# Fifty-one words of a written-out instruction order change place, in a kernel of block-sparse attention and a squared-ReLU layer

## The chip, the cores and the metric

The kernel runs on one core of a Trainium2 chip. Five engines work side by side, each with a queue of its own: PE (TensorE, matrix products; its weight loads, PEld, overlap them), DVE (VectorE), ACT (ScalarE), POOL (GpSimd) and SP (SyncE, which here only issues transfers and reads registers). Transfers are done by 16 DMA engines. The metric is the device time in microseconds of one execution. Beside the median of the timed runs there is one profiled execution, from which all rows of the profile come.

## The reference

Attention over 4 batches, 8 heads, 768 positions and 64 dimensions, with a mask in blocks of 32 positions: each block of queries sees its neighbours, the first and the last block, and three sampled blocks of keys; the first and the last block of queries see all keys. Its output, 3072 rows of 512, goes through a layer with a squared ReLU.

```python
mask = np.abs(blk_i - blk_j) <= window
mask = mask | (blk_i == 0) | (blk_j == 0) | (blk_i == n_blocks - 1) | (blk_j == n_blocks - 1)
for qb in range(n_blocks):
    for kb in sampled_blocks[qb]:
        mask[qb*block:(qb+1)*block, kb*block:(kb+1)*block] = True
...
attn = attn / (np.sum(attn, axis=-1, keepdims=True) + 1e-09)
x = attn_out.transpose(0, 2, 1, 3).reshape(B * S, H * D)
h = x @ w_in            # 512 -> 2048
r = np.maximum(h, 0.0)
return (r * r) @ w_out  # 2048 -> 512
```

## The kernel before, in words

The work is cut into some 1200 tasks. A *unit* is a pair of heads of one batch (units 0 to 3 are batch 0, 4 to 7 batch 1, and so on); a *tile* of the layer is 256 rows of one batch, written (batch, first row, 256).

Batches 0 and 1 are done densely: a unit's queries and keys are loaded, cast to bf16 (`cast_qk`, `cast_v`, line 121 on ACT, 123 on DVE and POOL), transposed (`transp` on PE, or by a DMA transpose, `transp_dma`, line 312), multiplied (`scores`, by way of `pair`, line 203), exponentiated on ACT (`exps`, L357), masked on DVE (`masks`, L364), multiplied with the values (`values`) and normalized (`normalize`, L407 and L410). The result is transposed into `xT` by PE (`x_transp`, and `x_evac` copies it out of PSUM) or by DMA (`x_transp_dma`, L437).

Batches 2 and 3 are done sparsely, in six *visits* each. The value rows of a batch are stored to memory (`v_store`, L533, `rows<-VB`) and read back selected: a window and the edge blocks by plain transfers of SP (`v_window`, L547 and L551), sampled blocks by an indirect transfer of POOL (`v_gather`, L573). Keys are selected on chip by copies whose place comes from registers (`k_gather`, L588 to L594, on POOL or DVE). The registers are filled by a read of the table `tab` (`blocks_of`, L556, shown as TENSOR_LOAD): the first reads for POOL, DVE and SP are made at the end of `table_rows` (task 25), and each later one at the end of the `k_gather` or `v_gather` that has used up the one before it. Then `s_scores`, `s_exps` (L619), `s_masks` (L626), `s_values` (L649), `s_normalize` (L655, L658) and `s_transp` (L662) follow.

The layer of a tile is `hidden` (16 columns of 128 in four groups of four, each in four tasks), `relu` (L703 on ACT, L705 on DVE), `square` (L714 on ACT, L716 on POOL), and `output` in eight parts, followed by `out_copy` and `store`. The last tiles' outputs are split into narrower pieces.

The order is written out by hand. The string `PROGRAM` lists all tasks as words: the letter is the engine (P for PE, V for DVE, A for ACT, G for POOL, S for SP), then comes the task's number, and after a slash the PSUM cell (0 to 3) that its result takes. Each engine does its words in the order in which they stand; what stands between two words of one engine that belong to other engines fixes only the order in which buffers are handed out.

```python
for word in PROGRAM.split():
    i, _, spot = word[1:].partition("/")
    t = tasks[int(i)]
    ...
    t.fn(names[word[0]])
```

Buffers of a pool (`qc` for cast keys and queries, `pT` for exponentials, `r` and `g` for the layer, `ys` for outputs) rotate; a task waits for the last reader of the buffer that it takes. The transfers that SP issues go through eight completion counters in rotation, so a transfer also waits until the one eight places before it has landed.

Of the kernel before, what the change touches and what calls it, by code (L numbers as in the profile page):

```python
# [25 lines left out]
def kernel(  # L26
# [751 lines left out]
    def T_(f, *args, **kw):  # L778
        return Task((lambda e: f(*args, e)), **kw)
# [102 lines left out]
    def visit(b, v, vw, acts):  # L882
        gs_ = [g for g in VISITS[v] if g]
        vb, kb = Buf("vg"), Buf("kg")
# [76 lines left out]
    for T in TILES:  # L961
# [35 lines left out]
        V29 A32 V35 P30/2 P36/0 P0/3 V31 V37 A1 P33/2 V34 P11/3 G46 P100/3 P104/1 A101 V43 A105 P44/2 P102/0 V45 P47/3 A103 V57 V109  # L997
        V48 V54 P58/3 P111/1 V59 P55/3 A112 P113/2 V56 P115/0 V41 A114 P4/3 P9/3 P125/1 V67 G64 P2/3 A116 P106/2 V3 G52 A126 P5/3
        P123/3 V107 A124 G74 P108 P65/1 P121/0 V110 V66 G63 A122 P68/3 P82/1 P84/2 V69 P131/3 S18 V83 A85 S28 S19 S42 S53 S20 P135/0
        A132 V49 P86/2 P117/1 V87 G60 A136 G73 V118 P61/3 P133/2 V62 P90/0 G38 P119 A134 P127/3 V91 G75 P168/0 A120 P15/2 V128 P39/2  # L1000
        G76 P10/1 A169 P12/1 P174/1 V153 V40 P129 P137/2 G78 V130 A175 P144/0 G70 P88/3 V138 P147/1 A145 V176 P139 A89 P71/0 V140 V72
        A148 P171/3 V170 P779/2 P780 A172 V146 P92/1 P187/0 P781 V93 A188 P782 V173 P50/3 P181/1 A783 V189 P177/0 V51 A182 G784 P141/2
        P772/3 V178 P773 A142 V149 G79 P184/1 P179 P774 V207 V180 A185 G22 V143 P94/0 P775 V183 P155/2 A95 P150/1 V776 A156 G785
        P158/0 A159 P161/2 V151 P786/3 V186 P787 A162 P215/0 V157 P152 P788 A154 P14/2 V160 P789 A216 P98/2 P190/1 S80 V163 S251 A99
        V790 S252 P212/0 A777 P164/2 A213 V191 G791 P793/3 A778 V165 P794 S81 P209/0 G792 S259 P192 P166 P795 A210 V167 S260 P796 V193
        V294 V217 G77 P822/2 A797 P823 V214 P197/1 P194/0 G799 P824 A198 P825 P816/3 A195 G254 V826 P817 P226/1 A798 S255 P818 V196
        A227 P200/2 P810/0 V264 P811 S267 A201 V211 P243/1 P819 S265 V256 P812 A244 P218/2 V228 P813 S257 A820 V199 P219 P800/1 V220
        A814 S261 V202 P240/3 P221 P801 A241 V262 P96/0 S263 P802 A222 V97 A815 V242 P237/2 P223/3 S268 P203/0 A238 V245 P803 S275
        V272 A224 S332 S276 P229/2 P204 P804 V225 A230 S273 P805 G266 A821 V231 P286/2 P806 A287 V205 P232/3 V239 A827 P206 P289/2
        P233 V270 P807 A290 V208 S271 V234 P296/0 A808 P246/2 V291 P235 S253 P247 V236 A297 V288 S437 P299/1 P828/3 V248 P829 A300  # L1010
        V280 P302/0 P830 V278 A303 P249 P283/1 P831 V250 S279 V298 A284 P314/2 P850/0 V832 P851 S277 A315 P844/1 V304 S281 P845 A833
        P311/3 V285 P852 P853 V258 A312 P846 V301 S269 P847 A854 V316 P292/3 S21 P862/2 V313 A848 P293 P305/0 V295 P863 G282 A855
        P308/1 P306 G849 S454 P864 A309 V307 P353/3 S436 P865 A354 P326/0 P856/1 V866 P857 A327 P320/3 P858 V310 A321 P323/2 V274
        P834/0 V355 A324 S438 P859 V322 S445 P347/3 P835 A860 S383 S444 V328 P317/2 S460 A348 V325 P350/1 S809 P318 P836 V349 A351
        V319 P329/3 A867 P334/1 V352 P330 P837 A335 V331 G447 V23 P356/2 S333 A861 G439 P340/3 P838 A341 G441 P839 G459 P362/1 P337/3
        S452 P357 G443 P840 S442 A338 G449 P841 A363 S434 P868/3 S450 A842 P359/1 P869 V342 A360 S446 V339 P374/0 S843 P870 V345 A375
        V358 S462 V336 P377/1 S448 P365/2 P871 V361 A366 V364 P343/0 S461 A378 P371/2 V367 S453 P344 P872 V346 A372 V376 P368/1 P398/0
        V373 P401/2 P369 A399 P873 V379 A402 V370 S469 S440 P380/0 P391/1 P381 V403 A392 P385/2 P874 V382 A386 V400 S384 P388/0 P16/1
# [3 lines left out]
        V424 P395 S471 P416/1 P930/2 A417 P899 V397 P931 A895 P410/1 V900 P932 P933 A411 P902/0 V430 A934 V501 P475/1 P903 A476 P912/2  # L1022
        V418 P488/1 P904 V415 A489 V412 P431/3 A901 P480/1 P913 V477 S497 S604 P432 P914 S620 V433 A481 G635 P915 S614 V482 P419/1
        G502 A916 P485/3 S538 P905 A486 P420 A935 P490/3 P478/2 V421 P906 G498 V487 A491 S435 V544 P918/1 A479 P907 V492 G545 P473/3
        P483/2 P908 A474 S605 A484 P909 G615 A917 P919 P493/3 G499 A910 S911 G619 P506/0 S621 P920 V494 A507 P7/2 S540 S500 P512/2
        P921 A513 V508 P946/0 P947 A922 P509/3 P503/2 P948 A510 G522 P949 S622 P952/1 A504 S518 S543 V950 P552/3 P953 A923 G542 P936/2
        V514 S877 V511 P555/0 S496 P937 G541 V523 A556 P938 S616 A553 V505 P954 P546/0 P955 S521 A547 P939 V956 P515/3 V548 P524/0
        V557 P549/1 P940 A525 G587 V516 A951 P941 S517 A550 P942 G625 A957 V551 P527/1 P964/3 G519 S626 P965 A528 V554 P943 G617 V529
        P958/1 A944 P966 G607 P967 P959 V968 P530/0 P533/2 G623 P960 A531 S629 P961 V588 S583 S608 A534 P558/3 G520 A969 P992/2 S628
        V609 G565 P993 A962 S581 S618 P986/0 V559 P987 A963 P994 S610 V526 P592/1 P988 A593 P995 G627 P989 S606 A996 P970/1 V990 S561  # L1030
        S560 P998/3 G997 P589/2 V532 P999 A590 P971 P595/0 G562 P1000 A596 P972 V535 V566 G585 P1001 P536/2 G631 P980/0 A1002 V537
        P981 G584 P973 V633 S539 P982 G611 V597 P567/2 P983 S632 A568 P974 G563 A991 V984 P975 S586 A1003 P598/2 P976 S624 A599 P573/0
        P977 A574 V600 S636 V594 P1020/3 A985 S663 S564 P1021 V978 P570/2 P1026/0 A571 P1022 V591 S945 P1023 S665 S634 V640 P576/2
        P601/1 A577 V575 P1027 A1024 S637 P1004/2 V572 V602 A1025 P641/3 P1028 G666 V569 P1005 S603 A642 V578 G638 P1006 S639 P1032/3
        G669 P653/1 P1029 A654 P1033 A1030 P1007 P646/1 P1034 A647 P1035 P579/0 A1036 P1008 V580 A1031 P643/1 P656/3 V670 P1009 S582
        A657 P1010 A644 S706 S686 V645 P648/1 P1014/3 A649 P658/0 P1015 A659 P651/1 P1011 V660 A652 V655 V650 P1016 V690 A1012 P1017
        P661/0 A1018 S1013 G691 S979 A1037 S668 P680/1 P677/3 V662 P1048/2 G1019 A678 P1049 P1054/0 A681 V679 P674/3 P1050 A675 P1051
        G667 P1060/1 V1052 P1055 P671/3 G688 P1061 P1056 A1053 P1062 P1057 A672 P1038/2 V1058 P1063 P1066/3 V682 A1059 P1067 V673
        P692/0 P1039 V676 A1064 V712 P1068 A693 P683/1 A1065 G713 P1069 V684 S708 S664 P698/0 P1040 A699 G710 P1041 S749 S685 A1070
        V700 P720/0 P701/1 G1071 P695/3 S751 S687 P1042 A721 V733 A702 P1043 A696 P714/0 P1044 A715 P723/1 V694 P1045 G734 S711  # L1040
        P1088/3 A1046 P1089 P1082/0 S689 A724 P1083 P717/2 P1090 A718 G755 P1072/1 P1091 S1047 P1084 G709 V756 A1092 S752 P1094/2
        P1095 A1093 P1085 P1096 V1086 P1073 P1074 V703 V716 P1097 V719 P1100/3 V697 P1075 V1098 P704/0 V725 A1099 P1101 S729 V705
        P741/2 P1076 A742 V722 S707 P1102 P760/2 P1103 A761 P726/0 S732 A1087 P766/2 P1077 V727 A1104 P1078 V762 S728 A767 G1105 P1079
        V768 S754 P763/2 P735/0 P1106/3 A764 G730 A736 P1107 V737 G731 P744/0 P1108 V743 A745 V765 P1109 G753 A1080 P1130/0 P738/2
        P1116/1 A739 P1117 P1131 V740 P1118 V746 P757/2 P1119 A758 P1110 V1120 P747/2 V759 P1132 V748 P1133 P1137/1 V1134 S750 P769/2
        P1111 A1135 G1136 V770 P1138 G1122 S771 P1123/2 P1124 P1139 G1121 S1081 P1140 P1125 A1141 P1126 P1112 V1127 G1142 P1113 A1129
# [37 lines left out]
```

## Time and profile before

| what | us |
|---|---|
| median of 3 runs | 261.69 (261.49 to 263.17) |
| span of the profiled execution | 256.7 |
| median less span | 5.0 |
| PE busy | 242.0 (94%) |
| ACT busy | 186.2 (73%) |
| DVE busy | 166.8 (65%) |
| POOL busy | 95.7 (37%) |

The span runs from the first to the last instruction that the profile shows; the 5.0 us beside it lie around it. A row of waits reads: engine, line, what it waited for, the sum in us, how many times, the longest. A row of a timeline reads: start and length in us, engine, line, operation, what is written from what, how many instructions, and in brackets the idle time before it with what ended it. A row of the chain reads: start, length, what. A row of windows gives for each stretch its length and then, engine by engine, busy us and count, followed by the granted clock of PE as a share of full speed, the busy share of the DMA engines and the GB/s moved.

### The profile page before, as it was taken

To read this page: it belongs to the slowest core of one execution; us is meant where nothing else is said; L and a number is where in the kernel's file an instruction comes from. 1 tells how busy PE (TensorE), PEld (TensorE's weight loads), DVE (VectorE), ACT (ScalarE), POOL (GpSimd) and SP (SyncE) were. 2 spreads that over 40 slices of the span, in tenths; PEclk is the share of its full clock that TensorE was granted. 3 is DMA by queue.
4 is the path that set the end of the run, shared out by engine and by line. 5 is a ranking of instruction groups with operands and counts; after the bars stand their busy time and mean duration, and the time that the engine had idled before them with its cause. 6 is when DMAs were issued, how large, how long until landed. Compare 5 with 4: busy or idle time off the path is not lost.

```text
span 256.7 us, 12046 instructions
## 1 busy us (share of the span) xinstructions
PE 242.0 (94%) x5265; PEld 182.8 (71%) x5265; DVE 166.8 (65%) x390; ACT 186.2 (73%) x219; POOL 95.7 (37%) x193
## 2 busy tenths in 40 slices
PE   7988999999999997979999999989999999999993
PEld 4667889769876776856966776667866765777683
DVE  7677987879789986855375677366475665731300
ACT  3899999999998798858857857758777466244430
POOL 2274534020426014708437784162815307060200
PEclk9999999999999999999999999999999999999998
DMA  6999999999789999599999999981843556142031
GB/s 192 371 275 200 195 217 216 213 257 216 228 242 177 262 220 254 113 195 238 259 220 198 227 241 188 277 152 28 251 73 78 153 137 151 43 124 82 3 116 55
DMA packets 63509, 47.09 MB, mean 183 GB/s; under 512 B 31455, under 2 KB 58464, under 8 KB 63456
## 3 DMA queue, kind: packets, MB, share of 16 engines
q1 hardware_dynamic: 58320, 37.61, 65.9%
q0 software_dynamic: 4448, 8.25, 16.0%
q8 instruction: 41, 0.67, 1.1%
q10 hardware_dynamic: 688, 0.46, 0.6%
q14 instruction: 12, 0.10, 0.2%
HBM read 35.51 MB, written 7.91 MB: 169 GB/s over the span
## 4 chain that ended last, share of the span: by engine, by line
PE 66%; DVE 9%; DMA 7%; issue 5%; POOL 5%; ACT 4%; SPq 3%; DVEq 1%; POOLq 0%; ACTq 0%
PE X L203 59%; DMA QKT<-qc 5%; PE X L649 4%; POOL qc L123 2%; PE X L395 2%; DMA VG<-rows 2%; ACT pT L357 2%; POOL VG L573 2%; SPq L312 1%; DVE QKT L123 1%; SPq L151 1%; PE X L305 1%; ACT r L703 1%; DVE pT L364 1%; DVE qc L123 1%
## 5 line engine op out<-in xcount | busy, mean ns | idle before, releaser
L203 PE MATMUL X<-xT,w_in_sb 64*128 64x256 bf16 x1536 | 99.4, 269 | 1.8 <-ACT g L714 1.8
L203 PE MATMUL X<-w_out_sb,g 64*128 64x512 bf16 (+3 forms) x960 | 94.8, 333 | 0.1
L203 PEld LDWEIGHTS <-w_in_sb 64*128 64x128 bf16 x1536 | 74.0, 94 | 13.6 <-DMA xT<-XS 1.9
L357 ACT ACTIVATE pT<-X 128x1024 bf16<-128x1024 f32 x72 | 70.7, 1033 | 8.0 <-PE X L203 7.2
L203 PEld LDWEIGHTS <-g 64*128 64x128 bf16 x960 | 41.0, 94 | 26.8 <-PE X L203 0.4
L619 ACT ACTIVATE pT<-X 128x768 bf16<-128x768 f32 (+1 forms) x56 | 41.6, 765 | 21.8 <-PE X L203 20.8
L714 ACT ACTIVATE g<-r 128x1024 bf16<-128x1024 f32 (+1 forms) x44 | 40.3, 931 | 13.8 <-DVE r L705 13.7
L705 DVE TENSOR_SCALAR r<-X 128x1024 f32<-128x1024 f32 x22 | 26.9, 1224 | 24.7 <-PE X L203 23.2
L364 DVE TENSOR_TENSOR pT<-pT,VG 128x1024 bf16<-128x1024 bf16 x60 | 39.5, 692 | 3.2 <-ACT pT L357 2.4
L716 POOL TENSOR_TENSOR g<-r 128x512 bf16<-128x512 f32 (+1 forms) x16 | 20.9, 1316 | 47.8 <-DVE r L705 18.8
L626 DVE TENSOR_TENSOR pT<-pT,MKS 128x768 bf16<-128x768 bf16 (+1 forms) x48 | 28.3, 618 | 12.5 <-ACT pT L619 12.4
L703 ACT ACTIVATE r<-X 128x1024 f32<-128x1024 f32 x26 | 27.5, 1070 | 10.2 <-PE X L203 9.0
L203 PE MATMUL X<-QKT 64*128 64x256 bf16 (+1 forms) x384 | 32.5, 254 | 2.5 <-DMA QKT<-qc 1.6
L573 POOL DMA_INDIRECT VG<-rows,idx x20 | 20.0, 1000 | 19.7 <-DMA rows<-VB 9.4
L203 PEld LDWEIGHTS <-QKT 64*128 64x128 bf16 x384 | 16.9, 97 | 7.5 <-issue 3.6
L123 POOL CAST VB<-vs 128x768 bf16<-128x768 f32 x10 | 8.8, 888 | 27.3 <-DMA vs<-in_v_dram 21.3
L123 POOL CAST qc<-ks 128x384 bf16<-128x384 f32 (+1 forms) x17 | 9.3, 576 | 24.3 <-DMA ks<-in_k_dram 22.1
L203 PEld LDWEIGHTS <-pT 64*128 64x128 bf16 x768 | 16.1, 94 | 2.6 <-issue 0.2
L203 PE MATMUL X<-VB,pT 64*128 64x65 bf16 x768 | 17.1, 190 | 0.0
L203 PEld LDWEIGHTS <-KG 64*128 64x128 bf16 x528 | 13.2, 95 | 5.4 <-issue 1.8
L121 ACT COPY ys<-X 128x1024 f32<-128x1024 f32 (+2 forms) x11 | 9.9, 904 | 9.0 <-PE X L203 7.7
L203 PE MATMUL X<-QKT,KG 64*128 64x64 bf16 x528 | 14.8, 190 | 1.6 <-DVE XS L658 1.0
(104 smaller groups left out, 205.8 us busy)
## 6 DMA issues: line engine op xcount, KB each, us to landing
vs<-in_v_dram SPq DMA_DIRECT2D x14, 384.0 KB, 4.7
ks<-in_k_dram SPq DMA_DIRECT2D x13, 384.0 KB, 4.8
qs<-in_q_dram SPq DMA_DIRECT2D x12, 384.0 KB, 4.8
out_dram<-ys SPq DMA_DIRECT2D x9, 512.0 KB, 4.9
VG<-rows SPq DMA_DIRECT2D x20, 132.0 KB, 5.1
w_in_sb<-in_moe_w_in_dram POOLq DMA_DIRECT2D x2, 1024.0 KB, 9.2
w_out_sb<-in_moe_w_out_dram POOLq DMA_DIRECT2D x4, 512.0 KB, 8.4
rows<-VB SPq DMA_DIRECT2D x2, 792.0 KB
```

The lines of the kernel that those rows point to most:

```text
L123: (V if e == "DVE" else G).tensor_copy(out=out, in_=in_)
L203: last = nc.tensor.matmul(out(r ^ crossed), lhsT(r ^ crossed, rows), rhs(r ^ crossed, rows), skip_group_check=True, **kw)
L357: A.activation(out=pT[:, :, 0:n], in_=stile.pop(a)[:, :, 0:n], func=AF.Exp, scale=scale)
L364: V.tensor_tensor(out=pT, in0=pT, in1=m[:, None].broadcast_to([P, 2, len(cs), w]), op=AOP.mult)
L573: G.indirect_dma_start(out=to[0:RS * HB], out_offset=None, in_=pairs, in_offset=bass.IndirectOffsetOnAxis(ap=idx[0:RS * HB, g - 1:g], axis=0))
L619: A.activation(out=pT[:, :, 0:n], in_=stile.pop((u, v, gs))[:, :, 0:n], func=AF.Exp, scale=scale)
L626: V.tensor_tensor(out=pT, in0=pT, in1=m[:, None].broadcast_to([P, 2, n]), op=AOP.mult)
L649: nc.tensor.matmul(po[i * D:(i + 1) * D, h, a * VW:(a + 1) * VW], pts[g][:, h, c * D:(c + 1) * D], val, start=a == 0 and c == 0, stop=c == ...
L703: A.activation(out=to, in_=src, func=AF.Relu)
L705: V.tensor_scalar(out=to, in0=src, scalar1=0.0, scalar2=None, op0=AOP.max)
L714: A.activation(out=g, in_=r, func=AF.Square)
L716: (G if e == "POOL" else V).tensor_mul(out=g, in0=r, in1=r)
```

## The change

One dependency is added: a gather of keys now names `table_rows` among the tasks that must stand ahead of it in the string. It adds no instruction.

```diff
-            kc[g] = T_(k_gather, b, v, g, get=[] if kc else [kb], deps=[ev[u][1, 0] for u in us] + [tb["slots"]] + list(kc.values()))
+            kc[g] = T_(k_gather, b, v, g, get=[] if kc else [kb], deps=[ev[u][1, 0] for u in us] + [tb["slots"], tb["rows"]] + list(kc.values()))
```

The rest is the string. Of its words 31 change their letter: 28 claims (`xt_claim`, `v_claim`, `mk_claim`, `raw_claim`, functions that issue nothing) go from S to V; `x_evac` 120 goes from A to V, `square` 963 from A to G and `square` 997 from G to A. PSUM cells are renumbered throughout. On the engines these tasks move against their neighbours, as far as the prediction speaks of them:

- PE: 127 and 129 (values and transpose of unit 2) later, 187 ahead of 92, 152 earlier; 408 (values) and 422 (scores) from behind 924 and 925 to ahead of them; 488 (`s_scores` of unit 11) from behind 912 to behind 906; at the end 1202 from ahead of 1212 to 1215 to behind them.
- DVE: 358 (`normalize`) ahead of 339 (`masks`); 633 (`cast_qk`) ahead of 537 (`s_normalize`); 640 (`k_gather`) from ahead of 575 and 572 (`s_masks`) to behind them.
- SP: 440 (`transp_dma`) from behind 453 to behind 446; 612 (a load) and 468 (`v_store`) from behind 464 and 456 or between them to ahead of both; 500, 622, 911 and 543 ahead of the loads 605 and 621; 632 (`transp_dma`) ahead of 539 (`s_transp`).
- Task 25 (`table_rows`) stands earlier in the string. Its arithmetic keeps its place on DVE; its register read on POOL goes from between the casts 457 and 455 to between the casts 449 and 463, its read on SP from behind 468 to between 384 and 630.

Also moved, each by a place or a few: 337, 391, 401, 960, 988, 970 to 972 and 1189 on PE; 40, 130, 138, 170, 183, 274 and 319 on DVE; 154, 363, 386, 423, 489 and 778 on ACT; 498 on POOL; 521 and 604 on SP.

The stretch around the store of value rows, cut from the string (before, then after):

```diff
-        P875 V451 A389 G463 P404/2 P884/1 V876 A405 P885 G467 P425/0 S630 P886 V406 A426 S464 P24/2 G465 P887 V26 P878/3 A888 P879
-        S468 G457 P428/0 P880 V25 A429 V427 P881 G455 P407/1 V396 V27 A882 P924/0 P925 A889 P408 S456 P422/3 P926 V409 A883 P890/2
-        V387 S612 P927 V393 A423 P891 S466 P413/1 V390 P892 A928 P893 G470 S495 S458 P896/3 A414 V894 P897 G472 P394/0 S613 A929 P898
...
+        P391/0 P388/3 V451 A392 V403 P16/2 P875 A389 P404/2 V876 P884/0 S384 P885 A405 P425/3 P886 P24/1 A426 P887 V406 P878/2 V26
+        V25 A888 P879 S630 P428/3 G463 P880 S612 A429 P881 G467 P407/0 A882 P408 G465 S468 V427 P422/3 V27 A889 V396 P924/2 G457
+        P925 A423 S464 V409 G455 P926 P890/0 A883 P927 P891 A928 P413/3 V387 S456 P892 V393 P893 V390 A414 P896/2 V894 P897 S466
+        A929 P394/1 G470 P898 V424 P395 S458 P416/3 P930/0 V397 G472 A417 P899 S604 P931 V900 V538 A895 P410/1 P932 P933 A411 V430
...
```

More of the change, by code (lines that the diff above doesn't have):

```diff
@@ L1001 @@
[L1001 to L1016, printed above, removed]
@@ new lines @@
+        V189 A182 V51 P141/2 G784 V178 P772/0 A142 P773 V149 P184/3 P179 P774 V180 A185 G79 G22 P94/2 P775 V143 P155/1 A95 V776
+        P150/3 G785 A156 P158/2 V151 P161/0 A159 P786/1 P152 P787 V183 V186 A154 P215/2 A162 P788 V157 P14/3 S80 P789 V160 A216
+        P98/3 P190/0 V163 A99 S251 S252 P212/2 V790 A777 P164/3 A778 V191 G791 P793/1 A213 S81 V165 P794 G792 P209/2 P192 P166 P795
+        A210 S259 S260 V167 V193 P796 V217 G77 P822/3 V383 A797 P823 P197/0 V214 P194/2 P824 A198 G799 P825 P816/1 A195 V826 P817
@@ new lines @@
+        S628 P995 A593 P970/2 V526 S618 A996 P989 G627 G562 P998/1 A997 V990 P971 S610 G585 P589/0 V532 P999 A590 P972 V535 S606
+        V566 P595/3 P1000 A596 S560 P1001 P536/0 V633 G631 G584 A1002 S632 P980/3 V665 P981 V537 P973 S539 P982 V597 P567/1 P983
+        A568 P974 V706 S586 V984 A991 P975 G611 A1003 S624 P598/0 G563 P976 A599 P573/1 S636 P977 A574 V600 S564 V594 P1020/3 A985
+        V978 P1021 P570/0 P1026/1 A571 V591 P1022 P1023 V575 S945 P576/2 P601/0 V572 A577 S634 V640 P1027 A1024 V637 P1004/2 A1025
@@ new lines @@
+        V719 S752 P1100/2 V697 P1075 V1098 P704/1 V725 A1099 P1101 V729 V705 P741/3 P1076 A742 V722 S707 P1102 P760/1 P1103 A761
+        P726/3 S732 A1087 P766/1 V727 P1077 A1104 V762 P1078 S728 A767 G1105 P1079 S754 P763/3 P735/2 P1106/1 A764 V768 G730 A736
+        P1107 P744/3 P1108 G731 V737 A745 V743 P1109 A1080 V765 G753 P1130/2 P738/3 P1116/0 A739 P1117 P1131 V740 P1118 V746 P757/3
+        P1119 A758 P1110 V1120 P747/3 V759 P1132 V748 P1133 P1137/0 S750 V1134 P769/3 P1111 A1135 G1136 V770 P1138 S771 G1122
@@ new lines @@
+        P1123/2 P1124 P1139 G1121 S1081 P1140 P1125 A1141 P1126 P1112 V1127 G1142 P1113 A1129 P1154/3 A1114 P1155 P1144/0 A1143
+        S1115 P1156 A1128 P1161/2 P1157 P1162 V1158 P1145 P1146 A1160 A1159 P1175/1 P1163 P1176 P1168/3 P1169 P1177 P1178 P1147
+        V1179 P1170 P1171 P1164 A1172 P1148 V1165 P1149 A1167 G1166 P1150 A1181 P1151 A1174 G1173 A1180 P1182/1 A1152 P1183 P1184
+        S1153 P1185 P1192/3 P1193 P1186 P1187 P1188 P1194 P1195 P1189 P1196 A1190 P1197 P1198 P1199 S1191 P8/2 V1200 P6/0 P1212/1
@@ L1052 @@
+        S1201 P1213 P13/2 P1214 P1215 P1202/3 P1203 P1204 P1216 P17/0 P1217 P1205 P1218 P1219 P1206 P1207 P1208 A1220 P1209 S1221
+        V1210 S1211
     """
```

70 lines of the change are left out of this document (34 added, 36 removed).

## The prediction

> **What bounds the kernel now.** First the page's shares, then the waits of TensorE, then the chain that ended last, then timelines of the engines named in it.
>
> ```profile
> PE 242.0 (94%) x5265; PEld 182.8 (71%) x5265; DVE 166.8 (65%) x390; ACT 186.2 (73%) x219; POOL 95.7 (37%) x193
> ...
> PE X L203 <- ACT g L714: 1.8, 1, 1.8
> PE X L203 <- DMA QKT<-qc: 1.6, 1, 1.6
> ...
> PE X L203 <- DVE XS L658: 1.0, 1, 1.0
> ...
> PE X L203 <- issue: 0.6, 1, 0.6
> ...
> PE X L203 <- DVE ys L123: 0.4, 1, 0.4
> PE X L203 <- DVE XS L410: 0.4, 1, 0.4
> PE X L649 <- DMA VG<-rows: 0.3, 1, 0.3
> ```
>
> PE is busy 94% and every other engine has room, so a reordering can only win what PE waits, and can lose whatever new wait it gives PE. These seven waits make 6.1 us; the rest of PE's waits lie in the start. Each is one wait at one place: 84.0, 97.5, 110.7, 145.3, 162.3, 167.7 and 250.0 us. The largest two hang on one chain:
>
> ```profile
> 99.28 0.90 POOL qc L123 x2
> 100.18 1.86 issue
> ...
> 102.17 1.73 POOL qc L123 x2
> 103.91 1.22 SPq L312
> ...
> 105.81 6.45 DMA QKT<-qc
> ...
> 112.39 10.01 PE X L203 x246
> ```
>
> The "issue" is a register read: POOL loads sampled block numbers (L556) between two casts, so the second cast, task 455, is late, so the transposes 456 and 466 of SP are late, so PE stands at task 488.
>
> ```profile
> L556 DVEq TENSOR_LOAD <-tab x11: 1400/1414/2602, 94.8 to 194.2; - x11
> L556 POOLq TENSOR_LOAD <-tab x11: 1387/1607/3452, 98.5 to 194.2; - x11
> L556 SPq TENSOR_LOAD <-tab x2: 1298/2107/2916, 99.6 to 197.1; - x2
> ```
>
> These rows give the shortest, median and longest read in ns: 1.3 to 3.45 us in which that engine's queue starts nothing.
>
> **The change part by part.** Of the 51 words, 28 are claims of buffers that go from S to V: they emit no instruction and cost nothing. The rest:
>
> *Start (to 57 us).* Tasks 127, 129, 152, 187 and the PSUM cell numbers change, and evacuation 120 goes from ACT to DVE. PE's waits there have other causes than these tasks (the masks and R built by DVE). I take 0, with 0.4 to either side, the size of the smaller waits listed above.
>
> *84 us.* The 0.36 us before scores 365 waits for normalization 358, which stood behind mask 339 on DVE. Now 358 goes first: -0.36. Task 339 has the next scores as cover; if that cover is gone, it costs its own 0.7 us or less.
>
> *97.5 us.* Task 924 waits for the transposes of 384. Tasks 408 and 422, which ran behind 924 and 925, now run ahead of them, inside the wait:
>
> ```profile
> 100.12 0.54 PE L203 MATMUL X<-VB,pT 64*128 64x65 bf16 x24
> 100.49 0.39 PE L203 MATMUL X<-QKT 64*128 64x256 bf16 x4
> 100.70 1.05 PE L203 MATMUL X<-xT,w_in_sb 64*128 64x256 bf16 x16
> ```
>
> From 100.12 to 100.70 is 0.58 us of work: -0.58, and 1.18 of the 1.76 remains (bounds: 0, if the exponentials before 422 are late, to -1.2, if 384 lands earlier because less stands before it on SP).
>
> *97 to 109 us, the register reads.* The word V25 (table_rows, which ends in the reads for POOL, DVE and SP) moves. POOL's read falls into an idle stretch after 81 us. SP's read moves from behind the store of value rows 468, where it was hidden behind a wait for 455, to a place ahead of 630, 612, 468, 464 and 456; load 612 and the store go ahead of transpose 464, and 440 goes four DMAs earlier.
>
> ```profile
> 93.86 2.53 SPq L437 DMA_TRANSPOSE xT<-XS  x2
> 96.49 1.07 SPq L149 DMA_DIRECT2D vs<-in_v_dram  x1
> 97.67 1.21 SPq L312 DMA_TRANSPOSE QKT<-qc  x1
> 98.98 0.53 SPq L533 DMA_DIRECT2D rows<-VB  x1
> 103.91 1.22 SPq L312 DMA_TRANSPOSE QKT<-qc  x1
> 105.19 0.58 SPq L151 DMA_DIRECT2D qs<-in_q_dram  x1
> ...
> 98.32 1.86 POOL L123 CAST qc<-qs 128x384 bf16<-128x384 f32 x4 [1.52 <-DMA QKT<-qc]
> 102.17 1.72 POOL L123 CAST qc<-ks 128x384 bf16<-128x384 f32 x2 [1.98 <-issue]
> ...
> 106.81 0.39 POOL L588 COPY KG<-QKT 128x256 int32<-128x256 int32 x1 [1.47 <-DMA QKT<-qc]
> ...
> 107.51 1.65 POOL L594 COPY KG<-QKT 128x64 int32 x6
> ...
> 109.11 0.33 PE L203 MATMUL X<-QKT,KG 64*128 64x64 bf16 x6
> ```
>
> POOL: four casts waited 1.52 us for the landing of 440 and end at 100.18; 455 then began at 102.17. Without the read it ends near 101.2 at the latest (two casts at half of 1.86), against 103.89. SP: from 96.39 a read of 1.3 to 2.9, then 1.07 + 0.58 + 0.53 + 1.21 of issue put 456 at 101.1 to 102.7 instead of 103.91, but now with a load and the store shortly ahead of it in the transfers. Gather 472 (L588 to L594) began when 456 had landed, 2.90 us after its issue, took 2.35 us, and scores 475 followed at 109.11, so 475 has no slack. The bounds for 475: -0.94 (all that PE brings) to +1.2 (the store and the load, 0.8 and 0.4 MB by their shapes, add as long a landing as three quarters of the read and issue they pass). I take -0.6, nearer to the SP sum.
>
> A rule of the Trainium skill speaks to this term: "DMA: Bandwidth & Descriptors", section "Latency and other measured facts", gives a tensor_load a floor of about 600 ns. The trace never shows less than 1298 ns. By the page's figure SP's read would cost 0.7 us less and 475 would come at the full -0.94.
>
> *110.7 us.* 488 moves from behind 912 to behind 906, about 15 tasks later; 466 has landed long before: -1.65. What is late next is 458 (one DMA later), needed by 485 about a microsecond after 488's old place; it gains from 455 as 466 does. Running sum: -2.25.
>
> *113 to 162 us.* PE has no wait here but "issue" 0.6, which no word touches: 0, bounds -0.6 and 0. Squares 963 (ACT to POOL) and 997 (POOL to ACT) swap:
>
> ```profile
> L716 POOL TENSOR_TENSOR g<-r 128x1024 bf16<-128x1024 f32 x5 | 9.5, 1893 | 15.9 <-DMA VG<-rows 10.6 <-ACT r L703 5.3
> L714 ACT ACTIVATE g<-r 128x1024 bf16<-128x1024 f32 x31 | 32.6, 1059 | 6.4 <-DVE r L705 6.3
> ```
>
> One costs +0.83 where the other saves 0.83; cast 627 and gathers 562 and 585 stand behind 963 on POOL, as the latter two stood behind 997. The consumers are output tasks some 3 us later: 0; without that cover 0.8. The loads 605 and 621 go behind 500, 622, 911 and 543; their casts run above 10 us later, so 0.
>
> A rule against this part is in the Trainium skill, "SBUF — State Buffer", section "SBUF: two separate sides": a DVE operation with two SBUF inputs locks out a POOL operation that reads SBUF. By it 963 could wait out the masks of L626 beside it, a few tenths each; the trace shows only that POOL's square takes 1.8 times ACT's.
>
> *162 and 168 us.* 601 waits 0.34 for a value window, and 653 waits 0.98 for normalization 602, which stands behind gather 640 on DVE, its register read, and masks 575 and 572:
>
> ```profile
> 163.18 0.29 DVE L588 COPY KG<-QKT 128x256 int32<-128x256 int32 x1 [1.59 <-DMA QKT<-qc]
> ...
> 163.60 0.70 DVE L594 COPY KG<-QKT 128x64 int32 x6
> 166.78 1.03 DVE L626 TENSOR_TENSOR pT<-pT,MKS 128x768 bf16<-128x768 bf16 x2 [2.49 <-ACT pT L619]
> 167.73 0.20 DVE L655 RECIPROCAL ss<-X 128x8 f32<-128x8 f32 x1
> ...
> 168.71 0.26 PE L203 MATMUL X<-QKT,KG 64*128 64x64 bf16 x6 [0.98 <-DVE XS L658]
> ```
>
> The row blames ACT for the 2.49, but the masks' exponentials were done; it is the read (2.60, the longest of DVE's). Now the masks go ahead of 640, into its 1.59 of waiting: 0.95 off (167.73 less 166.78). The read still stands between 640 and 602. With a usual read (1.41) another 1.19 goes. So 653 could begin 2.14 earlier with transpose 624 unmoved; PE could come 2.25 + 0.34 + 0.98 = 3.57 earlier. Transpose 624 itself moves, because 632 no longer stands behind 539, which waited for a normalization while the DMA engines had room:
>
> ```profile
> 103.00:105.00 2.00, 2.00 (x58) 1.82 (x56) 1.67 (x3) 2.00 (x3) 1.56 (x2) 1.00 0.00 0
> ...
> 154.00:157.00 3.00, 3.00 (x50) 1.83 (x46) 2.92 (x5) 1.47 (x2) 2.59 (x3) 1.00 0.64 150
> ```
>
> (The last two numbers of a row are the DMA engines' busy share and GB/s.) A transpose's issue (1.22) taken out of the way gives 1.2; that makes 3.34 at 653, and I take 3.2, since cast 633 now also stands ahead of that normalization.
>
> *250 us.* Task 6 waits 0.40 for copy 1200, whose cell it took; now 1212 to 1215 have other cells, and 1202, which takes that cell, stands behind them: -0.40.
>
> Sum: -3.2 - 0.4 = **-3.6 us**. The profiled span is 256.7; 261.69 less 256.70 is 4.99 us outside it, which I leave unchanged. 253.1 + 4.99 = **258.1 us**.
>
> **The rivals.**
> *The gather of batch 3 sets the time* (0.18). 624 lands no earlier, because the DMA engines are full from 105 to 154 us, and the read is again 2.60. Then 653 begins only 0.95 earlier, whatever PE won before; with the tail -1.35: 260.3. For it: what is won in the middle is waited for again at a fixed landing. Against it: the 0.64 share before 157, and the median read of 1.41.
>
> *Slower: SP's read ahead of the transposes* (0.18). SP sits in its read while the engines run dry, then load 630, load 612 and the store (384 + 384 + 792 KB by their shapes) transfer ahead of 464 and 456. With the longest read seen (3.45) and the 150 GB/s of the last row, 456 lands near 99.8 + 10.4 + 1.2 = 111.4, against 106.8: 475 stands 4.6 us longer. PE then keeps only 488's 1.65 and the tail's 0.40, and is at about +2.6: 264.3. It decides the sign where 456 lands later than about 109. Against it: 0.00 share at 103 to 105 in the row above shows that before has an idle stretch of its own in this place.
>
> *The change does not do what it says* (0.06): the words are mostly claims, and the PE moves swap one wait for another, so only the tail is left: 261.3.
>
> **How the numbers follow.** The forecast's case has 0.58. Its bounds: all terms at their best, -0.94 - 1.65 - 0.34 - 0.98 - 0.40 - 0.6 (145 us) - 0.4 (start) = -5.3, so 256.4; at their worst without a rival about -2, so 259.7. Range: 256.4 to 262.3, which takes in two rivals and leaves out the slower one and a little beyond either end. A change of under 1% (2.6 us) can hardly be told from none. Faster by over 1% (below 259.07): 0.52 of the forecast's 0.58 and 0.03 of the gather's case, 0.55. Slower by over 1% (above 264.3): two thirds of the slower rival, 0.12, and 0.04 of the forecast's case for a new wait of PE that no row shows, 0.16. Within 1%: 0.29.
>
> **What the profile after would show.** Right: no PE wait for QKT<-qc at 110; the wait at 97.5 us near 1.2; POOL's first read near 81 us; 455 ended by 101.5; PE's waits for L658, L410 and ys gone. Wrong: SP's read ahead of 630 with the DMA share near zero behind it, then PE waiting for KG at 475 (L588 to L594); a PE wait before 653 of over 1 us on QKT<-qc or DVE; new waits of PE on ACT in the first 57 us.

## The result, and the profile after

The changed kernel took 259.50 us (median of 4 runs, 258.59 to 262.51); beside it the kernel before took 261.77 (4 runs). The ratio is 0.9893 with a 95% interval of 0.985 to 0.9936: about 1% faster, -2.3 us by the medians and -2.8 by the ratio (an execution more than 1.5% above the fastest of its kernel counts in the medians and not in the ratio). The forecast was 258.1 us, with a range from 256.4 to 262.3.

The profiled execution of the changed kernel took 259.75 us, with a span of 258.0. So 1.75 us lie around the span, not the 4.99 that the prediction left unchanged; the later profiles of the two kernels show 1.7 to 1.8. By that measure the first profile of before (span 256.7) was an execution of about 258.5 us, 3.2 below the median that it stood for; this is inferred, since the lowest of the three timed runs beside it took 261.49. It would explain why the profile after has a *longer* span than the profile before although the kernel is faster: one profile is one draw out of executions that lie several microseconds apart.

The page's shares and the waits of PE after:

```profile
PE 244.6 (95%) x5265; PEld 183.7 (71%) x5265; DVE 166.6 (65%) x391; ACT 185.0 (72%) x218; POOL 94.9 (37%) x193
...
PE X L203 <- issue: 2.6, 6, 0.8
...
PE X L203 <- ACT r L703: 0.6, 1, 0.6
PE X L203 <- ACT ys L121: 0.6, 1, 0.6
```

Of the seven waits that the prediction started from, six are gone (for the transposes of 384, for QKT<-qc at 488, for L658, L410, ys and the value window). What was one wait for "issue" of 0.6 is now six of 2.6 us, and two waits for ACT are new. The chain that ended last is PE for 79% of the span, where it was 66%.

### The profile page after: what moved, and what is told of

It reads as the page before. It is cut to its first block, busy times and chain, and to the rows that moved or that the text cites. A ratio compares the mean times of both kernels' runs of the same rounds, so it can differ in the third digit from the quotient of the medians.

```text
span 258.0 us, 12039 instructions
## 1 busy us (share of the span) xinstructions
PE 244.6 (95%) x5265; PEld 183.7 (71%) x5265; DVE 166.6 (65%) x391; ACT 185.0 (72%) x218; POOL 94.9 (37%) x193
## 4 chain that ended last, share of the span: by engine, by line
PE 79%; issue 2%; ACT 2%; DMA 1%; DVE 0%; DVEq 0%; ACTq 0%
PE X L203 74%; PE X L649 5%; DMA out_dram<-ys 1%; ACT pT L357 1%; ACT r L703 0%; ACT ys L121 0%; DVE ys L123 0%; ACT pT L619 0%; PE X L424 0%; DVEq L123 0%; PE X L516 0%; ACTq L121 0%; ACTq L357 0%
## 5 line engine op out<-in xcount | busy, mean ns | idle before, releaser
L203 PEld LDWEIGHTS <-w_in_sb 64*128 64x128 bf16 x1536 | 75.3, 94 | 13.8 <-issue 3.0
L573 POOL DMA_INDIRECT VG<-rows,idx x20 | 19.5, 973 | 24.8 <-DMA rows<-VB 8.9
L203 PEld LDWEIGHTS <-pT 64*128 64x128 bf16 x768 | 15.3, 94 | 4.2 <-PE X L203 0.9
L203 PE MATMUL X<-QKT,KG 64*128 64x64 bf16 x528 | 15.4, 190 | 1.2 <-ACT r L703 0.6
```

What stands on the lines that cost most here:

```text
L203: last = nc.tensor.matmul(out(r ^ crossed), lhsT(r ^ crossed, rows), rhs(r ^ crossed, rows), skip_group_check=True, **kw)
L573: G.indirect_dma_start(out=to[0:RS * HB], out_offset=None, in_=pairs, in_offset=bass.IndirectOffsetOnAxis(ap=idx[0:RS * HB, g - 1:g], axis=0))
```

## The experiments

All kernels are edits of the string of words, except one. In the diffs a word moves from where it has a minus to where it has a plus. Times are medians; the ratio is to the kernel before on the same chip.

### Before, unchanged, once more

No edit.

> The kernel before, unchanged, profiled once more. Theory A: the first profile of before was a favourable execution; what lies around the span is about 1.8 us for both kernels, so this profile has a span near 260 us, and the seven waits of PE come again (1.8 at the transposes of 384, 1.6 at 488, 1.0 at L658), with 2 to 4 us more lost in stalls of PE that wait for nothing shown (issue). Rival B: the span is 256.7 again and 5 us lie around it; then the change lengthens the span by 1.3 us and shortens what lies around it.

Measured: 263.78 us (6 runs, 260.23 to 266.32), beside 259.94 for the same kernel (23 runs, 256.71 to 267.16); the profiled execution took 260.23 with a span of 258.4. The waits of PE:

```profile
PE X L203 <- ACT g L714: 1.8, 1, 1.8
PE X L203 <- DVE XS L410: 1.7, 1, 1.7
PE X L305 <- POOL qc L123: 1.5, 1, 1.5
PE X L203 <- DMA xT<-XS: 1.5, 1, 1.5
PE X L203 <- DMA QKT<-qc: 1.3, 1, 1.3
...
PE X L203 <- DVE XS L658: 0.8, 1, 0.8
```

Theory A holds in the main: 1.8 us around the span, the waits at 384, 488 and L658 come again with 1.8, 1.3 and 0.8. Its span was expected near 260; and the excess over the first profile is not in "issue" but in waits for loads, transposes and L410 (1.5, 1.5, 1.7). Rival B falls. The two sets of runs of one and the same kernel have a "ratio" of 1.0193 (1.0116 to 1.027): the interval does not cover how far sets of runs of this kernel lie apart, and a single comparison of under 2% shows little here.

### The changed kernel, twice more

No edit; the second on another chip.

> The changed kernel, unchanged, profiled once more. Prediction's sum (-3.6 us on 261.7): ratio 0.986. Theory A: ratio 0.987 to 0.992, span near 257 to 258, the stalls of PE that showed as issue (at tasks 930, 488, 993) come at other places or are gone, the waits at 97, 110 and 168 us stay gone. Rival B: the stalls come at the same tasks with the same length (1.0, 0.7 and 0.6 us), so they belong to the order of the instructions, and the changed kernel pays them each time.

> The changed kernel a third time, on one chip with the three below, and with before. If the gain is as in the runs so far: ratio 0.988 to 0.994. PE's stalls between products, if they come, lie at the instruction counts 4280 and 4791 or another 256 away; POOL's gather 472 begins behind 470 near 107 us, and PE meets 475 within 0.7 us of it.

Measured: 258.01 us (12 runs), ratio 0.9937 (0.9892 to 0.9982), span of the profile 255.5; and 261.87 (6 runs) beside 262.88 (23 runs), ratio 0.9893 (0.9822 to 0.9963), span 260.4. Three comparisons put the changed kernel 1.0 to 2.3 us below before by the medians (1.6 to 2.8 by the ratios), and each of their intervals ends below 1; the differences stay below the 1.9% by which two sets of runs of before differed. The first of these two missed its expected ratio (0.987 to 0.992), and in its profile PE waits again for L658 at 653 (0.70) and for the gathered keys at 475 (0.54). The second met its ratio and its stalls at the counts 4280 and 4791, which are explained below; gather 472 began at 108.29 in it, 1.14 us after 470 had ended, where near 107 and right behind 470 was expected. Here is scores 488 in the first profile after and in the first of these two:

```profile
117.38 0.30 PE L203 MATMUL X<-QKT 64*128 64x64 bf16 x8
118.23 0.24 PE L203 MATMUL X<-QKT 64*128 64x64 bf16 x4 [0.55 <-issue]
...
117.78 0.28 PE L203 MATMUL X<-QKT 64*128 64x64 bf16 x8
119.27 0.24 PE L203 MATMUL X<-QKT 64*128 64x64 bf16 x4 [1.21 <-issue]
```

PE stops after the eighth of twelve products, waiting for nothing that the profile shows; the third profile has 0.89 at the same product. This looked like rival B (the stall belongs to the new order). The next three experiments say otherwise.

### 488 alone

```diff
-        P912/2 V418 P488/1 P904
+        P912/2 V418 P904
...
+        P906 P488/1
```

with exponentials 489 behind 479; the PSUM cells of 918, 473 and 493 are numbered anew.

> Before, with only scores 488 (and its exponentials 489) at the places that the change gives them. If the wait of 1.65 us is removed for good: no PE wait for QKT<-qc near 110 us, ratio 0.994 (-1.65 us). If the DMA stream sets the time later (gather of batch 3): the wait moves to 601 and 653, where PE then waits up to 1.6 us longer, and the ratio is 0.998 to 1.002.

Measured: 261.16 us (6 runs, 256.27 to 264.70) beside 259.94; too few and too scattered for a ratio. In its profile PE has no wait for QKT<-qc near 110; its wait for L658 at 653 is 1.4 us, against 0.98 and 0.78 in the two profiles of before. So in this one profile the first theory is right on the spot, and the rival right in a third: some 0.5 of the 1.65 came back at 653. What this is in time these runs cannot tell.

### The register reads alone

Before, with casts 463, 467, 465 and 457, load 630, transpose 464 and store 468 behind the word V25, so that POOL's and SP's first reads fall as in the change.

```diff
-        V451 A389 G463 P404/2 ... G467 P425/0 S630 ... S464 P24/2 G465 ... S468 G457 P428/0 P880 V25
+        V451 A389 P404/2 ... P425/0 ... P24/2 ... P428/0 P880 V25 G463 G467 S630 S464 G465 S468 G457
```

> Before, with only the first register reads of POOL and SP at the places that the change gives them (POOL's after the cast 449, SP's between 384 and 630). Theory: cast 455 ends by 101.5 us instead of 103.9, the transposes 456 and 466 are issued 2 us earlier, and PE's wait at 488 shrinks from 1.65 us to 0 to 0.5: ratio 0.994 to 0.997. Rival (SP's read ahead of the transposes costs as much as POOL's saves): 456 is issued no earlier than 103, the wait at 488 stays above 1.2 us, or k_gather 472 keeps PE at 475; ratio 1.000 to 1.005.

Measured: 260.34 us (12 runs), ratio 1.0059 (1.0017 to 1.0101). POOL, then PE:

```profile
100.30 0.95 POOL L123 CAST qc<-ks 128x384 bf16<-128x384 f32 x2
107.67 1.01 POOL L573 DMA_INDIRECT VG<-rows,idx  x1 [6.42 <-DMA QKT<-qc]
108.68 0.41 POOL L588 COPY KG<-QKT 128x256 int32<-128x256 int32 x1
...
111.11 0.23 PE L203 MATMUL X<-QKT,KG 64*128 64x64 bf16 x4 [0.78 <-POOL KG L594]
...
117.61 0.61 PE L203 MATMUL X<-w_out_sb,g 64*128 64x512 bf16 x4
120.28 0.61 PE L203 MATMUL X<-w_out_sb,g 64*128 64x512 bf16 x4 [2.06 <-issue]
```

Cast 455 ends at 101.25, as the theory said, and the wait at 488 is gone entirely. But POOL then stands until 107.67 and begins its key gather (L588) only at 108.68, behind the gather of value rows 470 (L573); PE now waits 0.78 at 475 for that. The time fits the rival, with another mechanism than the prediction had; but 0.6% is within what two sets of runs of one kernel differ by, so the time alone settles nothing. In the last row PE stops for 2.06 us inside output 906, a task of the unchanged order: so the stall of "issue" does not belong to 488.

### Key gather ahead of the value gather

```diff
-        G470 P898 V424 P395 S458 P416/3 P930/0 V397 G472
+        P898 V424 P395 S458 P416/3 P930/0 V397 G472 G470
```

> The changed kernel with gather 472 of keys ahead of gather 470 of value rows on POOL. In both profiles of the changed kernel 472 begins only after 470, which waits for the store of value rows, though 455 and 456 are done 2 to 4 us earlier. Theory (the store, moved ahead of the transposes, holds the key gather through POOL's queue): 472 begins by 106 us instead of 107.3, PE's wait for POOL KG before 475 (0.64 us in the second profile of the changed kernel) goes, ratio against before 0.985 to 0.992. Rival (the DMA engines are full, 456 itself lands no earlier): 472 begins at 107 again and the time is that of the changed kernel, 0.990 to 0.994.

Measured: 259.79 us (6 runs) beside 262.96 (17 runs), ratio 0.9857 (0.9798 to 0.9916). POOL of the changed kernel first, then POOL and PE of this one:

```profile
99.12 0.95 POOL L123 CAST qc<-ks 128x384 bf16<-128x384 f32 x2
106.24 1.01 POOL L573 DMA_INDIRECT VG<-rows,idx  x1 [6.16 <-DVE XS L410]
107.26 0.41 POOL L588 COPY KG<-QKT 128x256 int32<-128x256 int32 x1
```

```profile
105.80 0.40 POOL L588 COPY KG<-QKT 128x256 int32<-128x256 int32 x1 [6.15 <-DMA QKT<-qc]
...
108.09 0.34 PE L203 MATMUL X<-QKT,KG 64*128 64x64 bf16 x6
```

The theory holds. In the changed kernel POOL stood 6.16 us in front of 470 (the release named, L410, was long past; what 470 needs beside its read registers are the value rows that store 468 writes). From the issue of that store to the start of 470 it is 9.0, 8.6 and 7.2 us in the three profiles of the changed kernel, 5.4 and 5.3 in the two of before, but 7.7 in "488 alone", which has the order of before here: what makes the store long is not shown. With 472 ahead, it begins with the landing of transpose 456, at 105.80, and 475 starts at 108.09 without a wait. The ratio is in the range expected (0.985 to 0.992); whether the move gains time against the changed kernel it does not show.

### 112 more PE instructions ahead of everything

The changed kernel; the extra products are warm-up work, so it does a little more than the others.

```diff
-    N_WARM, N_IDLE = 14, 14
+    N_WARM, N_SHORT, N_IDLE = 10, 32, 14
...
+    for _ in range(N_SHORT):
+        pair(lambda i: X[NX - 1][:, i, 0:32], lambda i, rows: warm[rows, 0:P], lambda i, rows: warm[rows, 0:32], start=True, stop=True)
```

> The changed kernel with 112 more PE instructions ahead of everything (4 wide warm-up products fewer, 32 narrow ones more), so that every later task starts 112 instructions further in PE's stream. Theory F (PE's stalls called issue come where a block of 256 instructions, 16 KB, ends before the next is fetched): stalls stay at the same count of instructions, 183 to 189 after a multiple of 256, and so lie 112 instructions earlier in the program: not inside 488 (its ninth product) but inside values 420 ahead of it; elsewhere likewise. Rival G (the stall belongs to 488 itself, a wait that the profile does not show): it stays in 488 after its eighth product, 0.5 to 1.2 us. Time: within 1% of the changed kernel by both.

Measured: 266.40 us (6 runs, 260.77 to 269.28) beside 262.96 (17 runs). Five of the six took 264.86 or more, which neither theory expected; they are too few for a ratio, and what makes them long was not found. The longest stall in the profile:

```profile
139.03 0.60 PE L203 MATMUL X<-xT,w_in_sb 64*128 64x256 bf16 x8
141.66 0.61 PE L203 MATMUL X<-xT,w_in_sb 64*128 64x256 bf16 x8 [2.03 <-issue]
```

488 runs through without a stall. Counting PE's products and weight loads from the first, the stall above comes at instruction 5811, between the tasks 964 and 965. Two later profiles of the unshifted order stall at the same count 5811, there inside scores 530, other work. The stall at 4791, too, lies inside 488 in some profiles and inside output 906 in the reads alone. Theory F holds in its main part (the count decides, not the task), G falls. F's single place, 420, did not stall. The trace also has the transfers that bring PE's instructions: 41 packets of 16 KB for 10,530 instructions, one per 256. For the block that is needed at count 4791 (17 x 256 + 439), over the profiles of unshifted orders, in order of where PE was when the packet began, with the longest pause of PE at that count (a usual one is 0.02 to 0.2):

```
profile of                    packet at   PE past 17 x 256 by   pause, us
loads later                     114.36          244                0.03
loads later, 602 first          112.04          244                0.02
before                          115.02          254                0.20
before, again                   115.78          260                0.63
602 first                       115.54          304                0.02
488 alone                       114.34          316                0.24
after                           115.68          322                0.74
squares back                    116.89          322                0.47
472 first                       113.81          324                1.06
after, third                    117.32          348                1.08
after, second                   116.79          392                1.40
472 and 602 first               116.34          416                1.76
reads alone                     117.92          439                2.43
```

The order is rough (0.63 at 260, 0.02 at 304), but every pause of over 1 us stands at 324 or more. Where PE waits for a block, it goes on 2.2 to 3.2 us after the packet begins, with two exceptions of 4.8 and 4.9. In the quiet stretch from 176 to 250 us the packets begin with PE 136 to 240 past the multiple, and PE never stalls there at these counts.

The order of before has such stalls too. The prediction's wait for "issue" at 145.3 us, which it left alone since no word touches it, is one: it comes at count 6063 (22 x 256 + 431), and the packet for the block due there began with PE 360 past 22 x 256. "488 alone" has two more, of 1.42 at 3770 and 1.15 at 4025.

### The loads 604 and 620 later

```diff
-        S604 P931 ... S620 V433
+        P931 ... V433 ... S435 S604 S620
```

> The changed kernel with loads 604 and 620 (384 KB each, cast only at 137 and 145 us) moved behind the transposes 435, so that the DMA engines carry 0.8 MB less between 107 and 118 us. Theory (the block of instructions after count 4791 comes late because the DMA engines are full when it is fetched): its fetch starts with PE at most 300 instructions past the block's multiple of 256 (322 and 392 in the two profiles so far), and the stall inside 488 (0.55 and 1.21 us) shrinks below 0.3. Rival (the start of the fetch does not depend on the load): the fetch starts at 320 to 390 again, and the stall stays. Time: 0 to -1 us against the changed kernel.

Measured: 261.78 us (12 runs) beside 262.88, ratio 0.9951 (0.9911 to 0.9991). The stretch from 108 to 116 us, in the changed kernel and in this one:

```profile
108.00:116.00 8.00, 7.74 (x186) 5.25 (x184) 5.37 (x18) 4.99 (x7) 4.07 (x12) 1.00 1.04 255
...
108.00:116.00 8.00, 7.62 (x172) 5.17 (x170) 5.95 (x18) 5.32 (x7) 3.43 (x12) 1.00 0.73 168
...
117.93 0.36 PE L203 MATMUL X<-QKT 64*128 64x64 bf16 x12
```

The share of the DMA engines falls from 1.04 to 0.73, the packet begins with PE at 244 instead of 322, and 488's twelve products run without a break: the theory holds at this block, both in this kernel and in the next one. But the time does not fall against the changed kernel (261.78 beside 261.87; 0 to -1 was expected); the loads come later, and the profile now has stalls of 1.25 and 1.51 us at the counts 5301 and 5811, whose packets began at 356 and 321 past their multiples. The stall was moved, not removed.

### Normalization 602 ahead of gather 640

```diff
-        V572 A577 S634 V640 ... V602
+        V572 A577 S634 V602 V640
```

alone, with 472 ahead of 470, and with the loads later.

> The changed kernel with normalization 602 ahead of gather 640 on DVE, so that 640's register read stands behind both. Theory (the read between 640 and 602 is what keeps PE at 653): 602 ends by 165.5 us, 653 begins when 640 ends near 166, and PE's wait for L658 (0.7 us in the second profile of the changed kernel, none in the first) is gone: 0 to -1 us against the changed kernel, ratio against before 0.986 to 0.993. Rival (landing of transpose 624 sets 653 alone): 653 begins no earlier than in the changed kernel, 167.9.

> Both: 472 ahead of 470 and 602 ahead of 640. If the two waits are independent, the gains add: 0.5 to 1.7 us below the changed kernel, ratio against before 0.983 to 0.990. If the DMA stream alone sets the middle of the kernel, the ratio is the changed kernel's, 0.990 to 0.994.

> The same, and normalization 602 ahead of gather 640 as in the run before. Theory: both gains, 0.5 to 1.5 us below the changed kernel; 602 ends near 165, 653 follows gather 640. Rival: 653 follows transpose 624 in any case, and the time is that of the changed kernel.

Measured: alone 258.97 us (6 runs, 258.50 to 260.27) beside 262.96, ratio 0.9863 (0.9821 to 0.9906); with 472 first 260.21 (12 runs), 0.9874 (0.9833 to 0.9915); with the loads later 260.74 (12 runs) beside 262.88, 0.9932 (0.9896 to 0.9968). DVE in the changed kernel, then in the first of these:

```profile
163.99 0.70 DVE L594 COPY KG<-QKT 128x64 int32 x6
166.93 0.21 DVE L655 RECIPROCAL ss<-X 128x8 f32<-128x8 f32 x1 [2.24 <-issue]
...
164.71 0.21 DVE L655 RECIPROCAL ss<-X 128x8 f32<-128x8 f32 x1
164.95 0.69 DVE L658 TENSOR_TENSOR XS<-X,ss 128x512 bf16<-128x512 f32 x1
165.56 0.28 DVE L588 COPY KG<-QKT 128x256 int32<-128x256 int32 x1
```

In the changed kernel the register read stands 2.24 us between the gather and the normalization; here 602 is done 2.2 us earlier. 653 itself did not come earlier by that: 168.68 in the first, 168.63 with 472 first, 166.37 with the loads later, and 167.93, 168.53 and 170.12 in the changed kernel's three profiles. In the first, PE came late and 653 did not wait, as that run's rival had it. All three lie below before; whether one beats the changed kernel, which had 0.9893, 0.9937 and, beside the same runs of before as the last, 0.9893, these runs cannot tell. The gains do not add: 472 and 602 first together have 0.9874, inside the range expected but no lower than 0.9857 and 0.9863 of each alone.

### The squares back on their engines

```diff
-        A962 P986/3 V559 P987 S608 P994 G963
+        A962 P986/3 V559 P987 S608 P994 A963
...
-        G627 G562 P998/1 A997
+        G627 G997 G562 P998/1
```

> The changed kernel with the two squares back on their engines (963 on ACT, 997 on POOL ahead of gather 562). By the prediction's sum the swap costs and saves 0.83 us off the path: same time as the changed kernel within 0.5 us. By the prediction's step at 168 us the swap lets cast 631 and transpose 632 go earlier: then 631 is cast 1.5 to 2.5 us later here, 632 and 624 follow, and 653 begins up to 1.2 us later.

Measured: 259.47 us (6 runs) beside 262.88, ratio 0.988 (0.9831 to 0.9929): the changed kernel's, within what can be told. POOL of the changed kernel, then of this one:

```profile
145.16 1.88 POOL L716 TENSOR_TENSOR g<-r 128x1024 bf16<-128x1024 f32 x1
...
150.30 1.46 POOL L123 CAST qc<-ks 128x384 bf16<-128x384 f32 x2
...
155.71 0.82 POOL L123 CAST VB<-vs 128x768 bf16<-128x768 f32 x1 [2.86 <-DMA vs<-in_v_dram]
```

```profile
150.70 1.89 POOL L716 TENSOR_TENSOR g<-r 128x1024 bf16<-128x1024 f32 x1 [2.43 <-ACT r L703]
...
155.09 0.97 POOL L123 CAST qc<-ks 128x384 bf16<-128x384 f32 x2
```

Without the swap POOL idles 2.43 us before 997 and casts 631 afterwards, at 155.09 instead of 150.30 (about 2 of the 4.8 us between the two is that PE was later in this execution: its task 998 began 2.1 us later). So the swap brings 631 forward by some 2 to 3 us, as expected. At 653 it may win up to 1 us: 996 to 653 takes 21.71 here and 20.39 to 20.97 in the changed kernel, and 653 waits 0.34 for 602 here, behind a register read of 2.89. In the time that is not visible. The square itself cost nothing that the time shows, as predicted.

## Why the prediction was right or wrong

The direction and the range were right; the size was forecast as -3.6 us, and the medians of three comparisons give -2.3, -1.9 and -1.0 (the ratios -2.8, -1.6 and -2.8). By the steps, with the start of PE's tasks in the two profiles of before and the three of after:

```
from task to task      before, again      after, second, third
30 to 779 (start)      19.77  19.31       19.60  21.22  19.44
283 to 924 (to 98 us)  39.80  41.21       39.55  39.13  40.97
924 to 475 (to 109)     9.86   9.86       10.83   9.94  10.98
475 to 918 (to 118)     9.30   9.35        8.72   9.44   9.03
918 to 996             28.66  27.90       29.25  28.24  29.65
996 to 653 (to 168)    21.64  23.19       20.39  20.97  20.45
653 to 1116 (to 219)   49.39  49.40       52.48  49.39  52.69
1116 to 1221 (end)     34.78  34.77       33.72  33.72  33.70
```

Added up, these profiles show no gain: from the start of task 30 to that of 1221 it is 248.9 us by the mean of before's two, and 249.2 by the mean of after's three. So they can say which waits went and which came, but they cannot share out the gain of the timed runs among the parts. That the sum came near it is in part luck, because a loss of 2.6 to 3.3 us that most profiles show behind 653 was not in it.

**Start.** Costed at 0; between executions it differs by more than between the kernels. Nothing to tell. (Of the words, 27 and not 28 are claims that change to V; nothing hangs on it.)

**84 us.** The wait for L410 is gone in two of three profiles and 0.63 in the third; before had 0.36 and 1.72. The step held.

**97.5 us.** Expected were 0.58 filled and 1.18 left. In two profiles nothing is left, in the third 1.25. The bound "384 lands earlier because less stands before it on SP" was the likelier end, not the middle: SP issued 384 at 91.14 instead of 93.86.

**The register reads.** Right up to the cast: POOL's read came at 77.7 us, 455 ended at 100.07. Wrong was the next term, "-0.6 at 475". It took from before that 472 follows the landing of 456. With 456 earlier and the store of value rows later, 470, which stands before 472 on POOL and waits for that store, came last instead: 472 began at 107.26, where it had begun at 106.81. The experiment with 472 first shows it. The prediction asked of the store only what it adds to the landing of 456, and not who waits for the store itself. It does not follow the slower rival either: SP's read took 1.74, and 456 was issued at 100.54.

**488.** The 1.65 went, in every profile that moves it. What the sum missed is what stood next: a block of PE's instructions that comes late. It stops PE in 488 for 0.55, 1.21 and 0.89 us, and at count 4280, just ahead of 475, by pauses of 1.10, 0.41 and 1.45 us. The stalls at 4280 make up most of what 924 to 475 lost; 408 and 422, 0.58 of work, had left that stretch as well. Two profiles of the unchanged order also stop at 4791 for 0.25 and 2.06 us, so the change does not create the stall; whether it makes it likelier, thirteen profiles do not settle.

**168 us.** The mechanism was right and the size was not: 996 to 653 got 1.8 us shorter by the means. The sum had 653 earlier by 3.2 in all; from the start of task 30 to 653 the means differ by 0.7 us (164.7 before, 164.0 after). DVE's read was again long (2.24) where the sum took the median, 1.41.

**After 168 us.** Here the prediction had nothing but the tail, and here most profiles of the changed order and its variants lose time. 653 to 1116 takes 49.39 or 49.40 in all four profiles of before's order (488 alone and the reads alone among them), and 49.39 in one of after; in the other nine of the changed order and its variants it takes 52.0 to 52.7. One place where it shows is exponentials 654, right behind 653. PE at 653 and ACT behind it, in the first profile after and in the second:

```profile
167.93 0.25 PE L203 MATMUL X<-QKT,KG 64*128 64x64 bf16 x6
...
169.52 0.49 ACT L619 ACTIVATE pT<-X 128x384 bf16<-128x384 f32 x1 [3.04 <-PE X L203]
```

```profile
168.53 0.26 PE L203 MATMUL X<-QKT,KG 64*128 64x64 bf16 x6 [0.70 <-DVE XS L658]
...
168.83 0.49 ACT L619 ACTIVATE pT<-X 128x384 bf16<-128x384 f32 x1 [2.44 <-PE X L203]
```

653's last product ends in the record at 168.18 and 168.80. So ACT starts 1.34 us after it in the one, and 0.04 in the other. ACT is not what is slow: the trace also has the times of the signals by which PE releases the others, as a rule 0.02 us behind the product's end, and in the first profile after they come late here. Four tasks of PE that end one after the other:

```
task    last product ends    signal
653          168.18          169.50
1029         168.62          169.59
1033         169.05          169.69
1007         169.92          169.94
```

PE goes on, and the signals are held and then come 0.09 to 0.25 us apart. DVE's squared-ReLU step 1052 starts 1.82 us late in the same way, so it is not one engine that reads late. The delay comes again at 699 (0.88) and 745 (1.40), and PE then meets ACT at 695 and 1116: the two new waits of 0.6. In the nine profiles that lose time, 12 to 20 of some 340 signals come more than 0.42 us late, the latest 1.7 to 2.5; in the other five none comes later than 0.41. The profiles part at 653 as well: PE waited there for 0.7 us or more in the five (before 0.98 and 0.78, 488 alone 1.4, the reads alone 1.0, after's second profile 0.70), and 0.34 or less in the nine. But the wait at 653 cannot be what starts it: 7 to 13 of the late signals come before 653, the first of them between 69 and 116 us (115.70 in the first profile after). In three variants (472 first, alone and with 602, and the 112 extra instructions) 654 itself starts without delay, and the loss is there all the same. Late signals stand in nine of ten profiles of the changed order and its variants and in none of four of before's order; what holds them, and whether the change brings it about, was not found and stays open. That the loss follows from them is a correlation and these few meeting places, not an experiment. The Trainium skill, "Perfetto Trace Analysis", section "Tensor Engine Instruction (MATMUL, LD_WEIGHTS)", says that TensorE's ends in a profile are estimates; here the fourth signal, 0.02 us behind its product, speaks for the recorded ends.

**250 us.** Sized too small: the wait for ys is gone (0.40), but 1116 to 1221 is 1.06 us shorter, in every unshifted profile of the changed order and its variants (33.70 to 33.74, against 34.77 to 35.06 in the four of before's order). The other moves of the tail (1189, 1202, 1216 to 1219) were not tried apart.

**Time around the span.** The term 4.99 was wrong, as told above. It stands outside the difference, so the forecast of the median, 261.69 less 3.6, did not suffer.

## What to carry to other kernels

A wait that a reorder removes is worth its length only if nothing that stood in its shadow comes next: list for every transfer that is moved who waits for *it*, on POOL's queue too, before counting what it lets go. Take a second profile of the unchanged kernel before summing terms of half a microsecond, and compare the time around the span with what the result file gives: here the three profiles of the changed kernel lie 4.9 us apart, more than the change brings. Where an engine starts late behind another, look for the time of the signal, not only for the end of the work. In a kernel whose tensor engine runs without a break, its instruction supply is a resource with a place in the sum.

## What the runs showed of the hardware

PE's instructions come in blocks of 256 (16 KB, 41 packets for 10,530). The packet for a block begins when PE has run 136 to 240 instructions past a multiple of 256 in the quiet stretch (176 to 250 us), and 174 to 439 past it where the DMA engines were full (share above 1) in the 4 us before; PE runs dry 428 to 442 past it, and then stands until mostly 2.2 to 3.2 us after the packet began: up to 2.87 us in one piece (472 first, count 6828). Moving 0.8 MB of loads out of the stretch brought the packet from 322 to 244 and took the stall away at that block. The Trainium skill, "Runtime: NRT & Kernel Launch", section "Instruction fetch mechanics", gives blocks of 256 instructions too, and calls the cost of crossing a block mostly hidden; in the quiet stretch the trace agrees, in the full one it does not.

PE's signals to other engines came 0.02 us behind the end of the product as a rule, but in nine of fourteen profiles 12 to 20 of some 340 came 0.42 to 2.5 us late, several close together, while PE went on; why is open.

A register read for six block numbers took 1.30 to 3.45 us in these traces, 1.4 to 1.5 as a rule; on DVE after gather 640 it took 2.60 in the first profile of before, and stood 2.24 us in the way in the changed kernel.
